# Attention slots and loads from unit 12 on placed later, and a planner that counts outstanding DMAs

## The chip, the cores and the metric

One core of a Trainium2 chip runs the kernel. The metric is the device time of one execution in microseconds (us). Several executions are timed; their median stands for the kernel. One further execution is recorded by the hardware profiler, and all views of the profile are of that one.

## The reference

Windowed attention with sink keys, and on its output a two-layer feed-forward net with a gate:

```python
scores = (q @ k.T) / 8           # batch 4, heads 8, sequence 768, head size 64
keep   = (key < 4) | (0 <= query - key < 128)
a      = softmax(where(keep, scores, -1e9))
x      = (a @ v)                 # heads side by side: 3072 tokens x 512
h      = x @ w_in                # 512 -> 2048
g      = h * sigmoid(beta * h)   # beta per column of h
out    = g @ w_out               # 2048 -> 512
```

All inputs and the output are float32; the kernel computes its products in bf16.

## The kernel before, in words

The 3072 tokens are cut into 8 **blocks** of 384 tokens (`NT`, `TT`). A block needs the attention of 4 **units**: unit n is one pair of heads for one half (384 queries) of one sequence. Units 4T to 4T+3 belong to block T, so there are 32 units, 0 to 31 (`NU`).

One unit goes through these steps:

- `load(n)` (line 392) reads q, k and v from DRAM into float32 staging tiles. All these loads are issued by SP, but for two at the start. Units 0 to 11 load one half in one way; units 12 to 15 load one half with 256-byte runs (six DMAs of 96 KB); from unit 16 on (`WHOLE`) a load fetches both halves of a pair of heads at once (six DMAs of 192 KB), so that only every second group of four units loads.
- `cast(n)` (line 438): GpSimd (POOL) casts q and k to a bf16 tile `qk16` (3 buffers) and v into `v_aug`. From unit 12 on (`XBAR`) a DMA transpose, issued by SP (line 453), turns `qk16` into `qkT`. Units before 12 are transposed by TensorE.
- scores by TensorE into `s_ps` (line 554; the sink keys at line 490), exponentials by ACT, masks by DVE, attention times v by TensorE (lines 593 and 604), division by DVE into `o_norm` (line 614). The sink keys are copied out of `qkT` by ACT (line 481).
- `transpose_out(n)` (line 619): from unit 12 on another DMA transpose of SP (line 623) puts `o_norm` into `xT`, the input of the feed-forward net.

A block's feed-forward part has 16 tiles of hidden columns. For each, TensorE makes 4 matmuls over `xT` (line 651, one for each of the block's four units), ACT a tanh (line 659) and DVE the gate (line 672). Then 48 projections (line 679; 16 for each of 3 groups of 128 tokens) go into a PSUM bank, ACT (once DVE) copies it to `out_sb` (line 687), and SP stores it (line 694).

**What sets the order.** The program is first written down in steps s = -6, -5, ...: each step has one hidden tile of a block, three projections of the block before, and whichever attention steps fall there. `FIRST[n]` is the step at which unit n starts; its scores come 3 steps later, its attention 5. `casts` gives the step of each cast, and calls of `load` are tied to certain casts. Every instruction becomes a node with a duration (`busy`, `lag`) and the nodes it depends on. `Prog.order` then plans: at each turn it takes, over all five engines, the node that could start first by these durations, among the next 160 nodes of an engine (40 for SP). So an instruction can be drawn ahead of others in the written order when the planner thinks that it will be ready. For DMAs the planner keeps one clock `dma_free`: a transfer occupies it for `lag` (size by a rate) and is landed 2000 ns after. `emit` writes each engine's instructions in the planned order, with semaphore waits. On the chip every engine, and SP's queue with all loads, transposes and stores in it, goes through its list strictly in that order.

Of the kernel before, what the change touches and what calls it, by code (L numbers as in the profile page):

```python
# [9 lines left out]
B, H, S, D = 4, 8, 768, 64  # L10
# [7 lines left out]
TT = 384  # L18
# [22 lines left out]
S_END = S_PIPE + (NT - 2) * NM  # L41

FIRST = {4: -6, 5: -4, 6: -2, 7: 1, 8: 22, 9: 26, 10: 30, 11: 34}
FIRST.update({n: 42 + 4 * (n - 12) for n in range(12, NU)})

XBAR, WHOLE = 12, 16

# [23 lines left out]
class Prog:  # L71
# [10 lines left out]

    ENGINES = ("pe", "act", "dve", "gp", "sp")
    AHEAD = {"pe": 160, "act": 160, "dve": 160, "gp": 160, "sp": 40}
    FIRST_DMA = 2000.0

    def __init__(self):
        self.nodes = []
# [64 lines left out]
    def order(self):  # L153

        for n in self.nodes:
            n.open = len(n.preds)
            for p in n.preds.values():
                p.succs.append(n)
        free = dict.fromkeys(self.ENGINES, 0.0)
        left = {e: [n for n in self.nodes if n.eng == e] for e in self.ENGINES}  # L160
        head = dict.fromkeys(self.ENGINES, 0)
        can = {e: [n for n in left[e] if n.open == 0] for e in self.ENGINES}
        placed = []
        dma_free = self.FIRST_DMA

        def best(e):
            q = left[e]
            while head[e] < len(q) and q[head[e]].place is not None:
                head[e] += 1
            if head[e] == len(q):  # L170
                return None
            last = q[min(head[e] + self.AHEAD[e], len(q) - 1)].id
            c = [n for n in can[e] if n.id <= last]
            if not c:
                return None
            n = min(c, key=lambda n: (max(n.ready, free[e]) + n.give, n.id))
            return max(n.ready, free[e]), n

        while len(placed) < len(self.nodes):
            found = [(*b, e) for e in self.ENGINES if (b := best(e)) is not None]  # L180
            start, n, e = min(found, key=lambda f: (f[0], f[1].id))
            free[e] = start + n.busy
            if n.dma is None:
                n.done = start + n.busy + n.lag
            else:

                dma_free = max(dma_free, start + n.busy) + n.lag
                n.done = dma_free + 2000.0
            n.place = start
            can[e].remove(n)  # L190
            placed.append(n)
            for s in n.succs:
                s.open -= 1
                early = s.id in n.soft or s.eng == e and not n.dma
                s.ready = max(s.ready, start + n.busy if early else n.done)
                if s.open == 0:
                    can[s.eng].append(s)
        return placed
# [64 lines left out]
def bass_streamingllm_window__then__act_swish_beta_kernel(  # L263
# [75 lines left out]
    def dve(t):  # L339
        return {"busy": t, "lag": 140.0}  # L340

    def transfer(size, rate):
        return {"busy": 500.0, "lag": size / rate}


    def select(out_ap, in_ap, patt, cmp, fill, base, cm, r, w):
# [45 lines left out]
    def load(n, v_queue="sp"):  # L392
        b, hp, half, pb = place(n)
        t0 = half * TT
        if n < XBAR:
            for name, src in (("q", q), ("k", k)):
                s = src[b, 2 * hp:2 * hp + 2, t0:t0 + TT, :].rearrange("h (p c) d -> p h (c d)", c=3)
                d = stage[name][pb][:, :, 3 * half:3 * half + 3, :].rearrange("p h c d -> p h (c d)")
                op("sp", lambda e, d=d, s=s: e.dma_start(d, s),  # L399
                   w=[(name + "_stage", pb, half, 0), (name + "_stage", pb, half, 1)],  # L400
                   dma=f"{name}{pb}_{half}", line=n < WHOLE, **transfer(2 * TT * D * 4, 329))
        halves = (0, 1) if n >= WHOLE else (half,)
        first, size = (0, 6) if n >= WHOLE else (3 * half, 3)
        for name, src in (("q", q), ("k", k), ("v", v)):
            if name != "v" and n < XBAR:
                continue
            for hh in range(2):
                s = src[b, 2 * hp + hh, 128 * first:128 * (first + size), :].rearrange(
                    "(c p) d -> p c d", p=128)
                op(v_queue, lambda e, hh=hh, s=s, name=name: e.dma_start(  # L410
                    stage[name][pb][:, hh, first:first + size, :], s),
                   w=[(name + "_stage", pb, x, hh) for x in halves],
                   dma=f"{name}{pb}_{half}{hh}", line=n < WHOLE and v_queue == "sp",
                   **transfer(size * 128 * D * 4, 220))

    w_in_src = moe_w_in.rearrange("(c p) f -> p c f", p=128)
    w_out_src = moe_w_out.rearrange("(m p) n -> p m n", p=128)
# [10 lines left out]
    def load_w(i):  # L428
        view, src, _ = w_piece(i)
        op("sp", lambda e: e.dma_start(view, src), w=[("wst", i % NW)], dma=f"w{i % NW}",  # L430
           line=True, **transfer(1 << 19, 389))

    def cast_w(i):
        view, _, dst = w_piece(i)
# [3 lines left out]
    def cast(n):  # L438
        _, _, half, pb = place(n)
        z = n % NQK  # L440

        def view(name):
            return stage[name][pb][:, :, 3 * half:3 * half + 3, :].rearrange("p h c d -> p c h d")

        for x, name in enumerate("qk"):
            op("gp", lambda e, x=x, name=name: e.tensor_copy(qk16[z][:, x, :, :, :], view(name)),  # L446
               r=[(name + "_stage", pb, half, hh) for hh in range(2)], w=[(name + "16", z)],
               busy=451.0, lag=100.0)
        op("gp", lambda e: e.tensor_copy(v_aug[pb][:, 3 * half:3 * half + 3, :, 0:D], view("v")),  # L449
           r=[("v_stage", pb, half, hh) for hh in range(2)], w=[("v_aug", pb, half)], busy=451.0,  # L450
           lag=100.0)
        if n >= XBAR:
            op("sp", lambda e: e.dma_start_transpose(
                qkT[pb][:, half, :, :].rearrange("p w (c x) -> p (w c) x", c=3),
                qk16[z][:, :, :, :, :].rearrange("p w c h d -> p (w c h d)")),
               r=[("q16", z), ("k16", z)], w=[("qkT", pb, half)], dma=f"t{pb}{half}",
               **transfer(2 * TT * 256, 150))


    def transpose_in(n, bank=tr_ps, name_of="tr", eng="dve"):  # L460
# [158 lines left out]
    def transpose_out(n, bank=tr_ps, name="tr", eng="dve"):  # L619
        _, hp, _, _ = place(n)  # L620
        z, T = n % NON, n // 4
        if n >= XBAR:
            op("sp", lambda e: e.dma_start_transpose(
                xT[:, hp, T * TT:(T + 1) * TT].rearrange("p (c x) -> p c x", c=3),
                o_norm[z][:, :, :, :].rearrange("p m h d -> p (m h d)")),
               r=[("o_norm", z)], w=[("xT", T, hp)], dma=f"x{z}", **transfer(TT * 256, 150))
            return
        bank16 = bank[:, :].bitcast(BF16)
        with P.together("pe"):
            for m in range(3):  # L630
                op("pe", lambda e, m=m: nc.tensor.transpose(
                    bank16[:, m * 128:(m + 1) * 128],
                    o_norm[z][:, m, :, :].rearrange("p h d -> p (h d)"), ident[:, :]),
                   r=[("o_norm", z), "ident"], w=[name], **pe(128))
        op(eng, lambda e: (e.copy if eng == "act" else e.tensor_copy)(
            xT[:, hp, T * TT:(T + 1) * TT], bank16[:, 0:TT]),
           x=[name], w=[("xT", T, hp)], **(act(TT) if eng == "act" else dve(275.0)))
# [40 lines left out]
    def project(T, t, m, bank, name, eng="act"):  # L678
        op("pe", lambda e: e.matmul(bank, g[T % 2][:, m, t * 128:(t + 1) * 128],  # L679
                                    w_out16[:, m, :], start=(m == 0), stop=(m == NM - 1)),  # L680
           r=[("g", T % 2, m), ("w_out", m // 2)], w=[name], **pe(NOUT))
        if m == NM - 1:
            z = n_out[0] % 4
            n_out[0] += 1

            if eng == "act":
                op("act", lambda e: e.activation(out_sb[z][:, :], bank, AF.Copy, bias=0.0,  # L687
                                                 scale=0.5),
                   x=[name], w=[("out_sb", z)], **act(NOUT))
            else:  # L690
                op("dve", lambda e: e.tensor_scalar(out_sb[z][:, :], bank, 0.5, None, ALU.mult),
                   x=[name], w=[("out_sb", z)], **dve(600.0))
            row = T * TT + t * 128
            op("sp", lambda e: e.dma_start(out[row:row + 128, :], out_sb[z][:, :]),
               r=[("out_sb", z)], dma=f"o{z}", **transfer(128 * NOUT * 4, 389))


    constants()
# [69 lines left out]
    for s in range(-6, S_END + NM):  # L768
# [27 lines left out]
        if s in casts:  # L796
            n = casts[s]
            cast(n)
            if n >= XBAR and n % 8 >= 4 and n + 4 < NU:
                load(n + 4)  # L800
        if s == FIRST[5] + 2:
            for x in range(4, 8):
                cast_w(x)
# [11 lines left out]
            load_w(15)  # L815
            load(12)
            load(13)
            load(14)
            load(15)
        if s == 34:  # L820

            first = {0: (mask_a[:, :], MASK_A), 1: (mask_b[:, 128:512], MASK_B)}
# [72 lines left out]
```

## Time and profile before

| | us |
|---|---|
| three timed runs | 233.91, 234.16, 235.10; median 234.16 |
| profiled execution, first to last instruction (span) | 234.5 |
| TensorE (PE) busy | 219.4 |
| ACT busy | 144.3 |
| DVE busy | 135.2 |
| POOL busy | 74.3 |
| bytes moved by DMA | 39.76 MB, 170 GB/s on average |

The profile gives the span of its execution; it has no other time of it, and the timed runs lie on both sides of that span. A page and its views are read as follows. A line such as `L679 PE MATMUL acc<-w_out,g` is a group of instructions of line 679 of the kernel on TensorE, which write `acc` and read `w_out` and `g`. `PE a <- DMA b: 2.3, 1, 2.3` in the list of waits says that TensorE's instruction a waited for the transfer b, 2.3 us in total, once, 2.3 us at the longest. In a timeline a line gives the start, the duration, the engine and the instruction; SPq is SP's DMA queue, whose durations are those of issuing, not of transferring. In a table of windows each line gives a stretch, its length, the busy time of PE, weight loads, DVE, ACT and POOL with the number of instructions, then TensorE's granted clock, the DMA engines' share and the GB/s that they moved.

### The profile page before, as it was taken

The page shows a single profiled execution, that of the slowest core. Times are in us where ns is not written, and L with a number is a line of the kernel's source. Part 1 is how long each engine was busy: PE and PEld are TensorE (multiplying, and loading weights), DVE is VectorE, ACT ScalarE, POOL GpSimd, SP SyncE. Part 2 cuts the span into 40 slices and gives each one's busy share as a digit, 9 for nine tenths or more (in the row PEclk, how much of TensorE's full clock was granted, in tenths as well). Part 3 has the DMA queues.
Part 4 walks back from the last instruction along what each step waited for, and adds up shares of the span by engine and source line. Part 5 has one row for each costly group of instructions (what it writes and reads, how often), then busy time and mean ns, then how long its engine had stood idle before and what let it go on. Part 6 is the DMA issues. An engine that isn't in the chain of part 4 may idle for free.

```text
span 234.5 us, 4406 instructions
## 1 busy us (share of the span) xinstructions
PE 219.4 (94%) x1690; PEld 119.7 (51%) x1714; DVE 135.2 (58%) x261; ACT 144.3 (62%) x249; POOL 74.3 (32%) x134
## 2 busy tenths in 40 slices
PE   4996989999969999999999999999999999999994
PEld 2653545555434555544555555555555555555541
DVE  5374999699632645632667547766656665343300
ACT  2385887697506674755875669767775874555421
POOL 7677777598313223214115343410000000000000
PEclk9999999999997999999999999999999999999999
DMA  6999999999699999998999886842220112111012
GB/s 158 269 373 264 318 328 227 321 388 197 147 212 226 177 218 255 203 231 201 215 232 214 182 169 164 160 84 64 62 64 17 45 20 62 45 48 45 19 71 89
DMA packets 96084, 39.76 MB, mean 170 GB/s; under 512 B 82736, under 2 KB 88896, under 8 KB 96064
## 3 DMA queue, kind: packets, MB, share of 16 engines
q1 hardware_dynamic: 93888, 39.07, 71.0%
q10 hardware_dynamic: 1632, 0.40, 0.8%
q8 instruction: 13, 0.21, 0.4%
q0 software_dynamic: 544, 0.02, 0.2%
q14 instruction: 7, 0.06, 0.1%
HBM read 27.30 MB, written 6.29 MB: 143 GB/s over the span
## 4 chain that ended last, share of the span: by engine, by line
PE 68%; SPq 20%; DMA 8%; issue 2%; POOL 1%; ACT 0%; POOLq 0%; ACTq 0%
PE acc L679 32%; PE h_ps L651 27%; SPq L410 13%; DMA v_stage<-in_v_dram 6%; SPq L399 4%; PE s_ps L554 4%; PE s_ps L604 3%; SPq L430 3%; DMA qkT<-qk 1%; PE s_ps L490 1%; PE s_ps L593 1%; PE h_ps L679 1%; POOL v_aug L449 0%; ACT out_sb L687 0%; POOL qk L446 0%
## 5 line engine op out<-in xcount | busy, mean ns | idle before, releaser
L679 PE MATMUL acc<-w_out,g 128*128 128x512 bf16 x345 | 94.0, 382 | 1.3 <-issue 0.5
L659 ACT ACTIVATE th<-h_ps,beta_half 128x384 f32<-128x384 f32 x104 | 58.9, 581 | 37.7 <-PE h_ps L651 35.8
L651 PE MATMUL h_ps<-xT,w_in 128*128 128x384 bf16 x416 | 79.4, 326 | 0.3 <-issue 0.2
L672 DVE SCALAR_TENSOR_TENSOR g<-th,h_ps 128x384 bf16<-128x384 f32 x104 | 56.0, 552 | 33.6 <-ACT th L659 32.0
L651 PEld LDWEIGHTS h_ps<-xT,w_in 128*128 128x128 bf16 x416 | 39.5, 98 | 30.3 <-DVE g L672 1.5
L679 PEld LDWEIGHTS acc<-w_out,g 128*128 128x128 bf16 x368 | 34.7, 98 | 34.0 <-issue 3.8
L570 DVE TENSOR_TENSOR E<-E,mask_all 128x1536 bf16<-128x1536 bf16 x20 | 19.4, 972 | 29.0 <-ACT E L561 29.0
L561 ACT ACTIVATE E<-s_ps 128x1536 bf16<-128x1536 f32 x20 | 28.9, 1447 | 5.9 <-PE s_ps L554 5.7
L446 POOL CAST qk<-q_stage 128x384 bf16<-128x384 f32 x32 | 18.3, 571 | 33.9 <-DMA qkT<-qk 33.3
L449 POOL CAST v_aug<-v_stage 128x384 bf16<-128x384 f32 x32 | 16.6, 529 | 35.0 <-PE s_ps L604 24.7
L687 ACT ACTIVATE out_sb<-acc 128x512 f32<-128x512 f32 x23 | 13.6, 597 | 14.6 <-PE acc L679 14.2
L651 PE MATMUL acc<-xT,w_in 128*128 128x384 bf16 x96 | 19.1, 327 | 2.6 <-DVE g L672 2.0
L604 PEld LDWEIGHTS s_ps<-v_aug,E 128*128 128x128 bf16 x384 | 17.1, 97 | 5.3 <-ACT E L524 0.7
L604 PE MATMUL s_ps<-v_aug,E 128*128 128x65 bf16 x384 | 19.4, 193 | 0.5 <-ACT E L524 0.4
L614 DVE TENSOR_TENSOR o_norm<-s_ps,rden 128x384 bf16<-128x384 f32 x32 | 17.8, 558 | 2.2 <-DVE rden L612 0.5
L446 POOL CAST qk<-k_stage 128x384 bf16<-128x384 f32 x32 | 18.3, 572 | 2.4 <-DMA k_stage<-in_k_dram 1.7
L659 ACT ACTIVATE th<-acc,beta_half 128x384 f32<-128x384 f32 x24 | 13.7, 580 | 5.9 <-PE acc L651 5.3
L672 DVE SCALAR_TENSOR_TENSOR g<-th,acc 128x384 bf16<-128x384 f32 x24 | 12.9, 547 | 3.8 <-ACT th L659 3.7
L524 ACT ACTIVATE E<-s_ps 128x768 bf16<-128x768 f32 x16 | 12.9, 809 | 2.2 <-PE s_ps L517 2.1
L475 DVE COPY qkT<-s_ps 128x768 bf16<-128x768 bf16 x10 | 9.5, 954 | 5.7 <-PE s_ps L468 5.7
L651 PEld LDWEIGHTS acc<-xT,w_in 128*128 128x128 bf16 x96 | 8.1, 98 | 8.5 <-DVE g L672 3.4
L481 ACT COPY k_sink<-qkT 64x4 bf16<-64x4 bf16 x32 | 6.1, 190 | 10.0 <-DVE qkT L475 9.0
(64 smaller groups left out, 155.0 us busy)
## 6 DMA issues: line engine op xcount, KB each, us to landing
out_dram<-out_sb SPq DMA_DIRECT2D x24, 256.0 KB, 2.3
q_stage<-in_q_dram SPq DMA_DIRECT2D x28, 192.0 KB, 4.2
k_stage<-in_k_dram SPq DMA_DIRECT2D x28, 192.0 KB, 4.2
wst<-in_moe_w_in_dram SPq DMA_DIRECT2D x8, 512.0 KB, 6.3
wst<-in_moe_w_out_dram SPq DMA_DIRECT2D x8, 512.0 KB, 9.1
v_stage<-in_v_dram SPq DMA_DIRECT2D x16, 192.0 KB, 4.2
v_stage<-in_v_dram SPq DMA_DIRECT2D x28, 96.0 KB, 5.3
q_stage<-in_q_dram SPq DMA_DIRECT2D x8, 96.0 KB, 3.3
```

What stands on the lines that cost most here:

```text
L410: op(v_queue, lambda e, hh=hh, s=s, name=name: e.dma_start(stage[name][pb][:, hh, first:first + size, :], s), w=[(name + "_stage", pb, x, ...
L446: op("gp", lambda e, x=x, name=name: e.tensor_copy(qk16[z][:, x, :, :, :], view(name)), r=[(name + "_stage", pb, half, hh) for hh in range ...
L449: op("gp", lambda e: e.tensor_copy(v_aug[pb][:, 3 * half:3 * half + 3, :, 0:D], view("v")), r=[("v_stage", pb, half, hh) for hh in range(2 ...
L561: op("act", lambda e: e.activation(E[z][:, :, :, :].rearrange("p c h x -> p c (h x)"), s_ps[:, :, :].rearrange("p (h b) x -> p h (b x)", h ...
L570: op("dve", lambda e: e.tensor_tensor(both, both, mask_all[:, half, :].unsqueeze(1).to_broadcast([128, 2, 768]), ALU.mult), r=[("E", z, 0) ...
L604: last=(x == len(kbs) - 1): e.matmul(av_ps[:, at + hh * D1:at + hh * D1 + D1], E[z][:, c, h2, col:col + 128], v_aug[pb][:, kb, hh, :], sta ...
L614: op("dve", lambda e: e.tensor_tensor(o_norm[o][:, :, :, :].rearrange("p m h d -> p (m h) d"), src[:, :, 0:D], rden[z][:, :].unsqueeze(2). ...
L651: op("pe", lambda e: e.matmul(bank, w_in16[:, c, m * 128:(m + 1) * 128], xT[:, c, T * TT:(T + 1) * TT], start=(c == 0), stop=(c == 3)), r= ...
L659: op("act", lambda e: e.activation(th[i % 3][:, :], bank, AF.Tanh, bias=0.0, scale=beta_half[:, m:m + 1]), x=[name], r=["beta"], w=[("th", ...
L672: op("dve", lambda e: e.scalar_tensor_tensor(g[T % 2][:, m, :], th[i % 3][:, :], 1.0, bank, ALU.add, ALU.mult), r=[("th", i % 3)], x=[name ...
L679: op("pe", lambda e: e.matmul(bank, g[T % 2][:, m, t * 128:(t + 1) * 128], w_out16[:, m, :], start=(m == 0), stop=(m == NM - 1)), r=[("g", ...
L687: op("act", lambda e: e.activation(out_sb[z][:, :], bank, AF.Copy, bias=0.0, scale=0.5), x=[name], w=[("out_sb", z)], **act(NOUT))
```

## The change

`FIRST` moves units 12 to 31 three steps later. The loads of units 14 and 15 and of all later pairs move from one place, or from the cast of the unit four before, to the cast of the unit two before (for the pairs that load in advance, a step of half a group later). The planner's DMA model is altered: the first DMA starts at 1300 instead of 2000, no more than 7 DMAs may be outstanding (a DMA starts only when the seventh before it has landed), issuing takes 525 ns for a load, 1400 for a transpose of q and k and 1250 for a transpose out, and the rates are others. No instruction's shape or number is touched.

```diff
-FIRST.update({n: 42 + 4 * (n - 12) for n in range(12, NU)})
+FIRST.update({n: 45 + 4 * (n - 12) for n in range(12, NU)})
...
-    FIRST_DMA = 2000.0
+    FIRST_DMA = 1300.0
+    DEPTH = 7
...
         dma_free = self.FIRST_DMA
+        landing = []
...
             n = min(c, key=lambda n: (max(n.ready, free[e]) + n.give, n.id))
-            return max(n.ready, free[e]), n
+            start = max(n.ready, free[e])
+            if n.dma is not None and len(landing) >= self.DEPTH:
+                start = max(start, landing[-self.DEPTH])
+            return start, n
...
                 n.done = dma_free + 2000.0
+                landing.append(n.done)
...
-    def transfer(size, rate):
-        return {"busy": 500.0, "lag": size / rate}
+    def transfer(size, rate, issue=525.0):
+        return {"busy": issue, "lag": size / rate}
...
    load, units 0 to 11, q and k:   rate 329 -> 300
    load, the others:               rate 220 -> 250
    load_w:                         rate 389 -> 380
    transpose of q and k:           rate 150 -> 240, issue 1400
    transpose out:                  rate 150 -> 280, issue 1250
    store of the output:            rate 389 -> 350
...
             cast(n)
-            if n >= XBAR and n % 8 >= 4 and n + 4 < NU:
-                load(n + 4)
+            if n in (12, 13):
+                load(n + 2)
+            if n >= XBAR + 2 and n % 8 in (6, 7, 0, 1) and n + 2 < NU:
+                load(n + 2)
...
             load(12)
             load(13)
-            load(14)
-            load(15)
```

More of the change, by code (lines that the diff above doesn't have):

```diff
@@ L400, in load @@
                    w=[(name + "_stage", pb, half, 0), (name + "_stage", pb, half, 1)],
-                   dma=f"{name}{pb}_{half}", line=n < WHOLE, **transfer(2 * TT * D * 4, 329))
+                   dma=f"{name}{pb}_{half}", line=n < WHOLE, **transfer(2 * TT * D * 4, 300))
         halves = (0, 1) if n >= WHOLE else (half,)
@@ L413, in load @@
                    dma=f"{name}{pb}_{half}{hh}", line=n < WHOLE and v_queue == "sp",
-                   **transfer(size * 128 * D * 4, 220))
+                   **transfer(size * 128 * D * 4, 250))
     w_in_src = moe_w_in.rearrange("(c p) f -> p c f", p=128)
@@ L430, in load_w @@
         op("sp", lambda e: e.dma_start(view, src), w=[("wst", i % NW)], dma=f"w{i % NW}",
-           line=True, **transfer(1 << 19, 389))
+           line=True, **transfer(1 << 19, 380))
     def cast_w(i):
@@ L456, in cast @@
                r=[("q16", z), ("k16", z)], w=[("qkT", pb, half)], dma=f"t{pb}{half}",
-               **transfer(2 * TT * 256, 150))
+               **transfer(2 * TT * 256, 240, 1400.0))
     def transpose_in(n, bank=tr_ps, name_of="tr", eng="dve"):
@@ L625, in transpose_out @@
                 o_norm[z][:, :, :, :].rearrange("p m h d -> p (m h d)")),
-               r=[("o_norm", z)], w=[("xT", T, hp)], dma=f"x{z}", **transfer(TT * 256, 150))
+               r=[("o_norm", z)], w=[("xT", T, hp)], dma=f"x{z}", **transfer(TT * 256, 280, 1250.0))
             return
@@ L694, in project @@
             op("sp", lambda e: e.dma_start(out[row:row + 128, :], out_sb[z][:, :]),
-               r=[("out_sb", z)], dma=f"o{z}", **transfer(128 * NOUT * 4, 389))
+               r=[("out_sb", z)], dma=f"o{z}", **transfer(128 * NOUT * 4, 350))
     constants()
```

## The prediction

> **What bounds the kernel now.** I read the view of cores first (one core, clock 0.992), then the page: TensorE is busy for 219.4 of 234.5 us, so what can be won is idle or slowed TensorE time. TensorE's waits name the largest piece, and its timeline places it.
>
> ```profile
> span 234.5 us, 4406 instructions
> PE 219.4 (94%) x1690; PEld 119.7 (51%) x1714; DVE 135.2 (58%) x261; ACT 144.3 (62%) x249; POOL 74.3 (32%) x134
> ```
>
> ```profile
> PE s_ps L490 <- DMA qkT<-qk: 2.3, 1, 2.3
> PE h_ps L509 <- DVE far_b L382: 2.0, 1, 2.0
> ```
>
> ```profile
> 67.53 0.33 PE L631 MATMUL s_ps<-ident,o_norm 128*128 128x128 bf16 x3
> 70.13 0.34 PE L490 MATMUL s_ps<-qkT,k_sink 128*128 128x384 bf16 x1 [2.27 <-DMA qkT<-qk]
> ```
>
> TensorE runs dry at 67.86 us and waits 2.27 us for the transposed q and k of unit 12. The 2.03 us wait is in the start-up, where nothing is edited. Windows of 1 us show what follows (the number behind POOL's count is the granted clock):
>
> ```profile
> 69.00:70.00 1.00, 0.00 (x0) 0.00 (x0) 0.00 (x0) 0.00 (x0) 0.00 (x0) 1.00 0.97 209
> 70.00:71.00 1.00, 0.87 (x3) 0.36 (x4) 0.00 (x0) 0.49 (x1) 0.77 (x2) 0.72 1.27 245
> 71.00:72.00 1.00, 1.00 (x5) 0.16 (x3) 0.00 (x0) 0.00 (x0) 0.19 (x1) 0.50 1.27 216
> 72.00:73.00 1.00, 1.00 (x10) 0.51 (x10) 0.00 (x0) 0.15 (x1) 0.00 (x0) 0.50 1.35 220
> 73.00:74.00 1.00, 1.00 (x4) 0.36 (x3) 0.00 (x0) 1.00 (x1) 0.00 (x0) 0.57 1.29 230
> ```
>
> The clock falls to half for 3.4 us; what is lost is 0.28 + 0.50 + 0.50 + 0.43 = 1.71 us. After that TensorE is busy in every window to the end. Why the transpose was late stands in SP's queue: it is issued at 66.60 us, behind 26 loads, without having waited itself.
>
> ```profile
> 45.02 2.98 SPq L410 DMA_DIRECT2D q_stage<-in_q_dram  x2
> ...
> 65.48 1.07 SPq L410 DMA_DIRECT2D q_stage<-in_q_dram  x2
> 66.60 1.32 SPq L453 DMA_TRANSPOSE qkT<-qk  x1
> 67.97 1.17 SPq L410 DMA_DIRECT2D k_stage<-in_k_dram  x2
> ...
> 91.76 2.08 SPq L453 DMA_TRANSPOSE qkT<-qk  x1
> 93.89 1.26 SPq L623 DMA_TRANSPOSE xT<-o_norm  x1
> ```
>
> The last view is the chain that ended last; TensorE's own spacing is read from it, 3.45/16 = 0.216 us for a projection matmul and 0.65/4 = 0.1625 us for a hidden one (the page's 382 and 326 ns are latencies that overlap).
>
> ```profile
> 219.65 0.65 PE h_ps L651 x4
> 220.30 3.45 PE acc L679 x16
> ```
>
> **The change part by part.** No instruction is added or removed; the edits alter the planner's numbers and the program order, and so each engine's written-out order. I compared the orders of the two kernels; positions below are counted in them.
>
> *The wait that goes.* In the new order the transpose of unit 12 (T12; likewise for other units) stands behind the loads of units 12 and 13 only. These end at 57.80 us in SP's timeline, and POOL's cast of unit 12 ends at 57.38, so T12 is issued at about 57.9 and lands 3.5 us later (as at 66.60), at 61.4. TensorE asks for it after five more projection matmuls than before: 67.86 + 5 x 0.216 = 68.9. The wait and its clock drop go: 2.27 + 1.71 = 3.98 us. With nothing else the span is 234.5 - 4.0 = 230.5.
>
> *What is late next.* Block 3's hidden matmuls (its first reads all of xT for units 12 to 15) started at 111.2 us, behind 42 projections of block 2 that fill TensorE from 100.1 on. Now they stand earlier while the attention slots stand three steps later, and the last of their four inputs, the output transpose of unit 15 (xT15), stands further back in SP's queue. When TensorE asks: from 67.86 to the fourth of these matmuls the new order has 75 projections (16.2), 67 hidden matmuls (10.9), scores of 5 units at 0.44 (2.2), 4 sink scores at 0.17 (0.7), and attention of 5 units (4 x 0.53 + 0.36 = 2.5): 32.5 us. The same sum over the old order from T12's wait to the end gives 157.4 against 161.2 - 1.7 = 159.5 measured, 1.3% of small waits; so 32.9, and TensorE asks at 100.75.
>
> When xT15 lands: behind T12 come 6 loads, T13, 6 loads, T14. With 0.53 us for a half-pair load and 1.3 for a transpose (rows between 54.65 and 66.60) that is 57.9 + 12 x 0.53 + 3 x 1.3 = 68.2. Between there and xT15 stand 24 whole-pair loads, T15 to T18 and T20, xT12 to xT14, and 5 output stores. Before, 24 such loads, 5 such transposes and 3 stores took SP from 65.48 to 93.89, 28.4 us, without waiting for an engine. Adding 3 x 1.24 and 2 x 0.57 gives 33.3: xT15 issued at 101.5. Its landing took 3.1 to 4.1 us between 94 and 98: 104.6 to 105.6. That is one end. The other comes from the bytes: 24 x 0.197 + 5 x 0.197 + 4 x 0.098 + 5 x 0.262 = 7.4 MB, and some 0.45 MB still under way at 68.2; the window from 72 to 96 moved 226 GB/s at a DMA share of 1.29. The old stretch moved 6.5 MB in 28.4 us, 229 GB/s; 7.85 MB at that take 34.3 us: landing at 102.5. The rows are near each other; I take 103.5, a wait of 2.75 us (1.75 to 4.85).
>
> On the way T13 and T14 wait for POOL's casts with the next loads queued behind them: cast 13 ended at 59.6, SP gets there at 62.4; cast 14 ended at 63.6 and slips by one transpose, SP gets there at 66.9. No loss.
>
> *Sum.* What TensorE has left then: 272 x 0.216 + 317 x 0.1625 + 15 units' scores (6.6) + 8 sink scores (1.4) + 15 units' attention (6.8) = 125.1, with 1.3% 126.7; and 3.1 us from its last matmul to the end (231.4 to 234.5). Span 103.5 + 126.7 + 3.1 = 233.3, so 1.2 us less than 234.5.
>
> *Block 4* is asked for 24.8 us after block 3 (191 instructions by the same spacing). xT19 is 19 loads, 4 qk transposes, 4 output transposes and 3 stores behind xT15: 5.7 MB, 24.9 us at 229 GB/s. So the second wait is near nothing, up to 2 us if SP keeps 0.73 us per load. In blocks 5 to 7 the last attention ends 5.3 to 5.7 us before the hidden matmul that needs it; normalising (about 1.3) and a transpose (2.6 median landing) take 3.9. Nothing, with at most 0.5 us a block.
>
> *Waits moved onto ACT.* ACT copies unit 16's sink keys when T16 has landed, ahead of the next tanh, which frees a PSUM bank for TensorE. ACT gets there at about 85.9; T16 is issued near 81.5 and lands 5.7 later (as T14 did): 87.2. Up to 1.3 us, and for T17 up to 2. TensorE has no cover for it, but it is not additional: it arrives so much later at a block 3 that waits for xT15 anyway. Without that wait it would cost its own 0 to 2 us.
>
> *Edits at nothing.* FIRST_DMA, rates, issue times and DEPTH act only through the order. Casts move on POOL, which is 32% busy. TensorE's order before 45 us is reshuffled too; the waits it could change there are 0.57, 0.76, 0.42, 0.49, 0.49, 0.32 and 0.40, so I bound it at 1 us either way, hidden behind block 3's wait if that stands.
>
> [...] The row is the half clock right after 2.27 us of idleness. [...] The second row is 226 GB/s at loads that write 256-byte runs. [...]
>
> **The rivals.** *A, full gain: 230.5 to 231.4.* Transfers keep up. For it: between 30 and 35 us the DMAs moved 336 GB/s, and the new order spreads loads between transposes. Against: those 336 were mostly longer rows, and from 65 to 90, where loads and transposes ran as they will here, it was 210.
>
> *B, slower: the new wait halves the clock as the old one did.* It needs one wait at block 3 (or 4) of about the length that did it before, 2.27. Price up to 1.71, less what falls into the wait itself. From a wait of 2.3 us on nothing is won (2.3 + 1.7 = 4.0); from 3.5 on it is slower by over 0.5%. With the late end, 4.85 + 1.7, span 234.5 - 4.0 + 6.55 = 237.0; at 4.1 + 1.7, 236.3. [...]
>
> *C, the change doesn't do what it says: T12 still late,* for a cast that slips; 234.5. Against: 7 us of slack.
>
> **How the numbers follow.** Forecast (wait comes back, clock stays) 0.48; A 0.24; B 0.25; C 0.03. The runs' median, 234.16, is 0.34 below the profiled span; the page gives no other time of that execution. So 233.3 - 0.3 = 233.0 us for the run; block 4's possible share moves me to 233.2. Range 230.0 (A, 230.5 less 0.34 and a little) to 236.0 (B with a wait of 4.1), leaving out the longer waits of B. Half a percent, about what a measurement here can tell from no change, is 1.17 us. Faster: A and 0.18 of the forecast, 0.42. Same: 0.24 of the forecast, 0.12 of B, and C, 0.39. Slower: 0.13 of B, and 0.06 of the forecast for a second wait at blocks 4 to 7, 0.19. The forecast's own range, without those, is 103.5 replaced by 102.5 and 105.6: 232.0 to 235.1.
>
> **What would show it.** Right: no TensorE wait on qkT near 68 us; T12 issued near 58; a wait of h_ps on the DMA of xT near 101, of 1.7 to 4.9 us; SP issuing without pause from 58 to 101. Wrong: xT15 landed before 100.7 (A); half clock behind 101 (B); waits in blocks 5 to 7, or small waits in the first 45 us grown by over 1 us.

## The result, and the profile after

The changed kernel takes 243.13 us (median of four executions, 241.53 to 244.38) beside 234.03 us (233.84 to 235.1) for the kernel before: a ratio of 1.0383, 95% interval 1.0324 to 1.0441. It is slower by 9 us. The profiled execution is the one of 244.09 us; its span is 242.4 us. Ratios leave out executions over 1.5% above the fastest of the same kernel; one of these, the run cover's at a granted clock of 0.66, is also the reason why that kernel's profile comes from a second run.

The page's first lines:

```profile
span 242.4 us, 4427 instructions
PE 224.0 (92%) x1714; PEld 119.7 (49%) x1714; DVE 136.7 (56%) x261; ACT 144.9 (60%) x249; POOL 71.0 (29%) x134
```

TensorE is busy for 4.6 us more than before, with the same instructions. Half clock explains some 3.4 us of it: it lasts 10.24 us in all (below), 3.41 before. The rest can't be read off, since the profile of before holds 1690 of the 1714 matmuls. The list of TensorE's waits from 60 us on (what waits, for whom, total us, times, longest):

```profile
PE h_ps L657 <- DMA xT<-o_norm: 5.2, 2, 2.9
PE s_ps L560 <- DVE o_norm L620: 0.3, 1, 0.3
```

The wait on unit 12's transpose (T12) is gone. In its place stand two waits of hidden matmuls on output transposes. TensorE's timeline shows that they are those of blocks 3 and 4:

```profile
101.80 0.84 PE L657 MATMUL h_ps<-xT,w_in 128*128 128x384 bf16 x3
105.00 0.99 PE L657 MATMUL h_ps<-xT,w_in 128*128 128x384 bf16 x5 [2.36 <-DMA xT<-o_norm]
...
131.07 0.65 PE L657 MATMUL h_ps<-xT,w_in 128*128 128x384 bf16 x3
134.61 1.78 PE L657 MATMUL h_ps<-xT,w_in 128*128 128x384 bf16 x5 [2.89 <-DMA xT<-o_norm]
```

Each time three matmuls go ahead on the inputs that have landed, and the fourth waits for the block's last unit (xT15, xT19). Windows of 1 us show the clock behind the waits (the number behind POOL's count):

```profile
106.00:107.00 1.00, 1.00 (x8) 0.39 (x9) 0.90 (x2) 0.98 (x2) 0.00 (x0) 0.74 0.75 139
107.00:108.00 1.00, 1.00 (x4) 0.46 (x3) 0.21 (x2) 0.94 (x1) 0.72 (x2) 0.50 1.01 191
...
134.00:135.00 1.00, 0.39 (x2) 0.23 (x3) 0.00 (x0) 0.00 (x0) 0.00 (x0) 0.50 1.21 257
...
139.00:140.00 1.00, 1.00 (x5) 0.45 (x4) 0.82 (x1) 0.58 (x1) 0.01 (x1) 0.50 1.32 260
140.00:141.00 1.00, 1.00 (x6) 0.47 (x4) 0.55 (x1) 0.30 (x2) 0.00 (x0) 0.69 1.14 324
```

Half clock lasts 3.41 us behind the first wait and 6.83 us behind the second. SP's queue tells why the transposes were late (start, time to issue, instruction):

```profile
57.07 1.32 SPq L459 DMA_TRANSPOSE qkT<-qk  x1
...
102.55 1.25 SPq L629 DMA_TRANSPOSE xT<-o_norm  x1
...
119.69 1.22 SPq L629 DMA_TRANSPOSE xT<-o_norm  x1
120.95 0.58 SPq L416 DMA_DIRECT2D k_stage<-in_k_dram  x1
121.58 1.13 SPq L416 DMA_DIRECT2D v_stage<-in_v_dram  x2
122.75 1.59 SPq L416 DMA_DIRECT2D q_stage<-in_q_dram  x2
124.38 1.74 SPq L416 DMA_DIRECT2D k_stage<-in_k_dram  x2
126.17 1.73 SPq L416 DMA_DIRECT2D v_stage<-in_v_dram  x2
127.94 0.84 SPq L416 DMA_DIRECT2D q_stage<-in_q_dram  x1
128.82 1.51 SPq L629 DMA_TRANSPOSE xT<-o_norm  x1
```

T12 goes at 57.07 us, 0.8 us before the forecast. xT15 goes at 102.55; xT19 (the last line) has ten whole-pair loads between it and xT18. Compared with the kernel before neither is late; there SP issued xT15 and xT19 later still:

```profile
105.73 1.21 SPq L623 DMA_TRANSPOSE xT<-o_norm  x1
...
132.28 1.26 SPq L623 DMA_TRANSPOSE xT<-o_norm  x1
```

What moved further is TensorE's question. Before, the hidden matmuls of blocks 3 and 4 began at 111.22 and 137.60 us:

```profile
111.22 1.46 PE L651 MATMUL h_ps<-xT,w_in 128*128 128x384 bf16 x8
...
137.60 1.46 PE L651 MATMUL h_ps<-xT,w_in 128*128 128x384 bf16 x8
```

Now they begin at 101.80 and 131.07, so 9.4 and 6.5 us earlier, while the two transposes are issued only 3.2 and 3.5 us earlier. They are late for the place that the planner gave to their readers. The chain that ended last goes through xT19:

```profile
127.23 1.35 ACT E L567
128.82 5.74 DMA xT<-o_norm
134.61 1.78 PE h_ps L657 x5
```

This view leaves out its shortest pieces, and it infers what released a transfer from the event that came last. Here it names ACT, but ACT is not what held xT19: DVE had written `o_norm` for unit 19 by 124.99 us, and SP came to the transpose when it had issued the loads ahead of it, at 128.78.

### The profile page after: what moved, and what is told of

It reads as the page before. It is cut to its first block, busy times and chain, and to the rows that moved or that the text cites. A ratio compares the mean times of both kernels' runs of the same rounds, so it can differ in the third digit from the quotient of the medians.

```text
span 242.4 us, 4427 instructions
## 1 busy us (share of the span) xinstructions
PE 224.0 (92%) x1714; PEld 119.7 (49%) x1714; DVE 136.7 (56%) x261; ACT 144.9 (60%) x249; POOL 71.0 (29%) x134
## 4 chain that ended last, share of the span: by engine, by line
PE 72%; DVE 11%; DMA 7%; ACT 4%; SPq 3%; issue 1%; POOL 0%; ACTq 0%; POOLq 0%
PE acc L685 29%; PE h_ps L657 26%; PE s_ps L610 4%; DMA xT<-o_norm 3%; DVE g L678 3%; DVE E L541 3%; PE s_ps L560 3%; PE acc L657 3%; DVE qkT L481 2%; SPq L416 2%; DMA k_stage<-in_k_dram 2%; DMA v_stage<-in_v_dram 2%; ACT E L530 2%; PE h_ps L685 1%; PE s_ps L474 1%
## 5 line engine op out<-in xcount | busy, mean ns | idle before, releaser
L685 PE MATMUL acc<-w_out,g 128*128 128x512 bf16 x368 | 99.5, 382 | 0.0
L657 PE MATMUL h_ps<-xT,w_in 128*128 128x384 bf16 x416 | 84.4, 336 | 5.3 <-DMA xT<-o_norm 5.2
L665 ACT ACTIVATE th<-h_ps,beta_half 128x384 f32<-128x384 f32 x104 | 60.1, 581 | 44.1 <-PE h_ps L657 41.7
L657 PEld LDWEIGHTS h_ps<-xT,w_in 128*128 128x128 bf16 x416 | 40.8, 100 | 40.1 <-DMA xT<-o_norm 6.3
L685 PEld LDWEIGHTS acc<-w_out,g 128*128 128x128 bf16 x368 | 33.9, 98 | 32.7 <-issue 4.3
L452 POOL CAST qk<-q_stage 128x384 bf16<-128x384 f32 x32 | 16.5, 517 | 39.9 <-DMA q_stage<-in_q_dram 18.7
L455 POOL CAST v_aug<-v_stage 128x384 bf16<-128x384 f32 x32 | 16.1, 519 | 22.2 <-PE s_ps L610 11.8
L452 POOL CAST qk<-k_stage 128x384 bf16<-128x384 f32 x32 | 17.2, 539 | 17.4 <-DMA k_stage<-in_k_dram 16.7
```

What stands on the lines that cost most here:

```text
L657: op("pe", lambda e: e.matmul(bank, w_in16[:, c, m * 128:(m + 1) * 128], xT[:, c, T * TT:(T + 1) * TT], start=(c == 0), stop=(c == 3)), r= ...
L665: op("act", lambda e: e.activation(th[i % 3][:, :], bank, AF.Tanh, bias=0.0, scale=beta_half[:, m:m + 1]), x=[name], r=["beta"], w=[("th", ...
```

## The experiments

The letters here are those of the experiments, not the prediction's. Theory **W**: the new order puts output transposes behind loads on a transfer queue that the planner believes faster than it is; blocks 3 and 4 wait for them, and each wait brings a stretch at half clock. Rivals: **D**, the transfers are behind as a whole, wherever the matmuls stand; **E**, the reshuffled first 45 us cost the time (TensorE idles 6.38 us between 5 and 60 us, 4.54 before); the later **slots and loads** cost it; **C**, the clock alone costs it. Ratios are against the kernel before, run beside each on the same chip; its medians there were 234.54, 235.35 and 234.24 us.

**late_xt: the planner told that output transposes land 4 us later.**

```diff
-                n.done = dma_free + 2000.0
+                n.done = dma_free + 2000.0 + n.late
...
-  dma=f"x{z}", **transfer(TT * 256, 280, 1250.0))
+  dma=f"x{z}", late=4000.0, **transfer(TT * 256, 280, 1250.0))
```

> The changed kernel, but the planner is told that an output transpose lands 4 us later than it reckons. So block 3's hidden matmuls stand 8 us of TensorE work later, block 4's 4 and block 5's 7; T12 stays early. Theory W (TensorE waits at blocks 3 and 4 for output transposes that the planner believed landed, and each wait halves the clock): both waits and the half clock go, span about 232.5, time 232 to 234. Rival D (the transfers as a whole have become too slow; the wait only shows first at blocks 3 and 4): the waits come back one block later, time 239 or more. Rival E (the new order of the first 55 us is what costs): that order is kept here, time 241 or more.

Measured 233.54 us, ratio 0.9962 (0.9931 to 0.9994); span 231.3. The list of TensorE's waits from 60 us on is one line, with no transpose in it:

```profile
PE h_ps L659 <- DVE g L680: 0.3, 1, 0.3
```

xT19 goes at 118.63 us with thirteen whole-pair loads fewer ahead of it, block 4's matmuls stand 3.8 us of TensorE work later, and the DMAs moved 206 GB/s from 83 to 109 us and 199 from 109 to 135, no faster than in the changed kernel (206 from 83 to 105, 202 from 105 to 134.6). So the transfers are not behind as a whole: D falls. TensorE's order is the changed kernel's up to block 3, so the new order of the first 45 us was kept: E falls as the main cause.

**planner_only: the kernel before with the new DMA model alone.**

```diff
+    DEPTH = 7
...
-  **transfer(size * 128 * D * 4, 220)
+  **transfer(size * 128 * D * 4, 250)
```

> The kernel before with the new DMA model alone: slots from step 42 and loads as before. Block 3's hidden matmuls stand as early as in the changed kernel, but T12 stands behind 24 loads and not 12. Theory W: xT15 has 24 loads and 6 transposes behind T12, is issued near 99.4 and lands near 102.5, when TensorE asks (102.4): wait of 0 to 1 us at block 3, about 1 at block 4, time 234 to 238. If the slots' shift of three steps is what costs, 234 or less. If the planner alone does the harm, 241 to 244.

Measured 243.87 us, ratio 1.0363 (1.0315 to 1.0411). My figure for W missed: I had taken the slots to be part of the cause. The model alone does all the harm, at other places: T12 is as late as before (65.39 us), four waits on qkT of 0.35 to 1.45 us follow, and one at block 4, for an xT19 that goes at 130.71:

```profile
134.41 1.58 PE L657 MATMUL h_ps<-xT,w_in 128*128 128x384 bf16 x5 [4.83 <-DMA xT<-o_norm]
```

Block 4 thus goes on at the same time as in the changed kernel (134.61), and from there to the end it takes 108.0 us (107.8). In the two orders nearly the same stands ahead of xT19 on SP: 42 whole-pair loads and 11 transposes of q and k here, 43 and 12 there. That accounts for the two times being so near; that like amounts on SP make like landings was not tested by itself.

**slots_loads_only: the kernel before with the later slots and loads, the old DMA model kept.**

```diff
-FIRST.update({n: 42 + 4 * (n - 12) for n in range(12, NU)})
+FIRST.update({n: 45 + 4 * (n - 12) for n in range(12, NU)})
...
-            if n >= XBAR and n % 8 >= 4 and n + 4 < NU:
-                load(n + 4)
+            if n in (12, 13):
+                load(n + 2)
...
```

> The kernel before with the slots three steps later and the loads moved, but the old DMA model. Block 3's hidden matmuls stand where they stood before, T12 behind 26 loads as before, and TensorE asks for it 1.1 us of work later. Theory W: the wait on T12 shrinks from 2.3 to about 1.2, no waits at blocks 3 and 4: time 232 to 234. If the shift of slots is what costs: 238 or more.

Measured 235.54 us, ratio 1.0042 (1.0002 to 1.0081), 1.5 us above W's figure: of waits on transfers, 0.97 us for an xT at 110.05 and 0.21 for a qkT are left. The slots and loads cost 0.4%, not 4%. It has 47 whole-pair loads ahead of xT19, more than the changed kernel's 43, and no wait at block 4, whose matmuls stand 9 us of TensorE work later.

**half_bytes: the changed kernel, whole-pair loads fetching only their first half** (the second half of each such pair's q, k and v is not loaded).

```diff
+                part = 3 if n >= WHOLE else size
...
-                    stage[name][pb][:, hh, first:first + size, :], s),
+                    stage[name][pb][:, hh, first:first + part, :], s),
```

> The changed kernel in the same order, but the loads of whole pairs (from unit 16 on) fetch only the first half of each sequence; the other half of the staging tiles keeps what was there, so that part of the computation uses old data. Theory W with the transfer rate as the limit of SP's queue: 2.4 MB less before xT15, which is issued near 96 and lands near 99, before TensorE asks at 102.6: no wait at block 3 or 4, span 232 to 235. Rival I (SP's issuing itself is the limit, whatever the size): xT15 is still issued at about 102 and the waits stay, span 240 to 243.

One execution, 233.52 us, span 231.8, with no wait of TensorE after 60 us. The instructions and their order on SP are unchanged, yet xT15 goes at 98.61 and xT19 at 122.38 us (102.55 and 128.82 in the changed kernel). xT19 also lands 2.5 us after its issue there, and 5.7 in the changed kernel. SP was held back by what it had already sent, not by its own issuing. The loads' runs of 256 bytes were halved with their bytes; the run does not tell these two apart, and it is a single execution.

**late_b4: late_xt's delay for block 4's transposes alone.**

```diff
-  dma=f"x{z}", late=4000.0, **transfer(TT * 256, 280, 1250.0))
+  dma=f"x{z}", late=4000.0 if T == 4 else 0.0, **transfer(TT * 256, 280, 1250.0))
```

> The changed kernel, in which the planner takes block 4's output transposes alone (xT16 to xT19) to land 4 us later than its model says. Block 3's hidden matmuls stay where the change put them, block 4's move back by 3.7 us of TensorE work. Theory W (each wait on an output transpose costs its own length and half of the stretch at half clock that follows it): block 3's wait of 2 to 3 us with 3.4 us at half clock stays, block 4's 2.9 us and the 3.4 us lost in 6.8 us at half clock go: 243.1 - 2.9 - 3.4 = 236.8, taken as 235.5 to 238. Rival D (the queue is simply behind, and a wait removed at block 4 comes back at a later transpose): 240 to 243. Rival L (block 4 carries all of the loss, block 3's wait is absorbed later): 233 to 235.

Measured 238.07 us, ratio 1.0144 (1.0079 to 1.0209), 0.07 us above W's range. Block 3's wait stays (2.32 us at 105.08, then 3.4 us at half clock); block 4's is gone, for xT19 goes at 125.05 with six loads ahead of it in place of ten. Of the 4.2% between the changed kernel and late_xt, block 4 carries 2.4 points and block 3, once block 4 is mended, 1.8 (each to within some 0.9).

**early_old: late_xt with the old order of the first 45 us** (limit and new rates only from unit 12's loads on, and only for transposes the new rates).

```diff
-            if n.dma is not None and len(landing) >= self.DEPTH:
+            if n.dma is not None and n.id >= self.deep and len(landing) >= self.DEPTH:
...
+            P.deep = len(P.nodes)
             load(12)
```

> The planner of before for everything up to unit 12's loads, so that the first 45 us keep the old order; from there the slots at 45, the moved loads, the limit of seven and the new times of the transposes, the old rates of the other transfers, and xT taken to land 4 us later. Theory W: no wait on an xT or qkT transpose after 60 us, full clock, 232.5 to 234, the same as the run late_xt within 0.7 us. Theory E (the new order of the first 45 us costs the 1.8 us by which TensorE's early waits grew): 231 to 232, 1.5 us or more below late_xt's 233.5.

Measured 233.54 us, ratio 0.9943 (0.9907 to 0.9979), span 231.5: the same as late_xt. The early order is worth nothing that shows. This is the fastest version of the study, but its interval and late_xt's overlap.

**after_old_start: the changed kernel with the old order of the first 45 us.** As in early_old the planner of before orders everything up to unit 12's loads; from there all of the changed kernel's numbers hold, its load rate of 250 too, and there are no 4 us.

> The changed kernel with the old order of the first 45 us: block 3's hidden matmuls stand after 83.3 us of TensorE work and block 4's after 108.4, as in the changed kernel (83.7 and 108.4). Theory W: the end is set by when xT15 and xT19 land, so time saved early is given back as longer waits there: 241.5 to 243.5. Theory E (the early order's 1.8 us adds to the waits): 240 to 241.4. If it falls below 239, the early order takes part in the waits at blocks 3 and 4, which neither theory says.

Measured 243.5 us, ratio 1.0343 (1.0259 to 1.0427). In the profile (span 239.1) TensorE waits for ScalarE and VectorE ahead of block 3 (1.50 and 0.76 us at 95 to 97 us, with half clock behind them) and comes to block 3 when xT15 has landed; ScalarE had itself waited 2.85 us for a qkT at 95.00; at block 4 it waits as before:

```profile
133.58 0.99 PE L659 MATMUL h_ps<-xT,w_in 128*128 128x384 bf16 x5 [2.52 <-DMA xT<-o_norm]
```

The ratio can't be told from the changed kernel's (1.0383, 1.0324 to 1.0441), though early waits are shorter. With early_old beside late_xt, E falls: the 1.8 us that it named do not show in either pair.

**old_rates: the changed kernel with the planner's old rates; the limit and the new issue times stay.**

```diff
-                   **transfer(size * 128 * D * 4, 250))
+                   **transfer(size * 128 * D * 4, 220))
...
-               **transfer(2 * TT * 256, 240, 1400.0))
+               **transfer(2 * TT * 256, 150, 1400.0))
...
-  **transfer(TT * 256, 280, 1250.0))
+  **transfer(TT * 256, 150, 1250.0))
```

> The changed kernel with the planner's old transfer rates (220 for loads in place of 250, 150 for transposes in place of 240 and 280, 329 and 389 for the rest), but its limit of seven and its longer issue times kept. Block 3's hidden matmuls then stand after 88.2 us of TensorE work (83.7 in the changed kernel, 91.9 in late_xt) and xT15 is issued one place earlier; block 4's stay at 108.2. Theory W with the rates as the part that misled the planner: no wait at block 3 or under 1 us, at block 4 one of 0 to 3 us with 3.4 us at half clock: 234 to 239. Rival (the limit of seven or the longer issue times misled it, the rates didn't): 241 to 244.

Measured 234.73 us, ratio 1.0005 (0.9967 to 1.0042), with no wait on a transfer after 60 us. The rates are what misled the planner. Which of them was not told apart: those of loads, of both transposes, of weights and of stores went back together.

**no_limit: the changed kernel with DEPTH at a thousand.**

```diff
-    DEPTH = 7
+    DEPTH = 1000
```

> The changed kernel with the limit of seven lifted to a thousand, so that the planner issues loads ahead again; its new rates and issue times kept. Unit 12's transpose then stands behind more loads, as in the kernel before, block 3's hidden matmuls after 85.9 us of TensorE work and block 4's after 106.6. Theory W (the rates misled the planner, whatever the limit): the wait on unit 12's transpose of some 2 us comes back and waits at block 3 or 4 stay: 238 to 244. Rival (the limit is what does the harm): 233 to 236.

Measured 247.12 us, ratio 1.0573 (1.0472 to 1.0675): further up than W's figure, and the opposite of the rival. With the new rates the limit helps by some 4 us. Without it T12 is late again (66.35 us, a wait of 1.23), and beside 1.43 us at block 3 and 3.41 at block 4 TensorE waits 3.37 us at 91.37 for ScalarE, which I hadn't foreseen: ScalarE had waited 4.21 us for a qkT at 89.68, so this too is the queue's.

**cover and cover_again: the changed kernel with matmuls that do nothing of use in the places of the two waits.**

```diff
+    COVER = {3 * NM: 14, 4 * NM: 24}
...
+            for _ in range(COVER.get(i, 0)):
+                cover(i)
             for c in range(3 if i < 2 else 0, 4):
```

> The changed kernel, in the same order, with extra matmuls (128x384, 0.164 us each) put ahead of the first hidden group of block 3 (14, 2.3 us) and of block 4 (24, 3.9 us), into the same bank, which the real group then starts afresh; the planner counts them as no time. TensorE works where it waited. Theory C (half clock comes from TensorE's idleness): full clock after block 3, 1.7 us won there; block 4 is asked for at 130.0, with the cover at 133.9, and xT19 lands at 134.6 as before, so a wait of 0 to 1 us stays and the 6.8 us at half clock, 3.4 us lost, go: 238.5 to 240.5. Rival (the half clock has another source, the traffic of transfers for one): it comes at 105 and 134 as before, 242 to 245.

> The kernel of the run cover once more, for a profile at full clock: its timed executions took 240.1, 241.0 and 241.0 us of span at clocks of 1.0, 0.998 and 0.993. Theory C with a cover of the right size: no wait above 1 us before blocks 3 and 4, clock 0.998 or more, and the span is then 239 to 241 because xT19's landing at 134 to 135 us sets block 4's start whatever the clock does before it. Rival O (the cover is too long: the transposes land before it ends, and its 6.2 us are paid as work): xT15 or xT19 lands 1 us or more before the cover's end, and the last wait is none. Rival S (something later than block 4 takes the time back): a stretch after 145 us with 1 us or more of idle TensorE that the changed kernel's profile doesn't have.

cover took 242.69 us, ratio 1.0347 (1.0261 to 1.0433): theory C had 238.5 to 240.5, and misses. The second run, with 243.81 us and a span of 241.9 (239 to 241 expected), gives the profile. The clock is full (1.00 in the mean, against 0.979 and 0.986 in the changed kernel's two profiles), so in this kernel idle TensorE is what halves it; but the time stays. TensorE's timeline around block 4:

```profile
129.72 4.06 PE L674 MATMUL h_ps<-xT,w_in 128*128 128x384 bf16 x24
133.62 0.65 PE L657 MATMUL h_ps<-xT,w_in 128*128 128x384 bf16 x3
135.20 0.99 PE L657 MATMUL h_ps<-xT,w_in 128*128 128x384 bf16 x5 [0.93 <-DMA xT<-o_norm]
...
146.06 0.32 PE L496 MATMUL s_ps<-qkT,k_sink 128*128 128x384 bf16 x1 [1.17 <-ACT E L567]
```

TensorE was at block 4 1.35 us earlier (129.72 against 131.07) and still could not start before 135.2: xT19's landing sets that. And behind the changed kernel's half clock this one meets the next wait: from 141 to 160 us TensorE is idle for 1.75 us, in the changed kernel for none. The view names ScalarE, but ScalarE had waited 1.89 us for a qkT itself (at 144.04), so it is a transfer again, and rival S's stretch after 145 us came in part. From block 4's fourth matmul to the end it takes 106.7 us, in the changed kernel 107.8: there 6.0 us of that stretch run at half clock, 3.0 us lost, and they are worth 1.1. By after_old_start, with full clock in that stretch and 105.5 us, they are worth 2.3; its order is a little different.

**after_again: the changed kernel, profiled once more.**

> The changed kernel once more, for a second profile: its four executions took spans of 239.8 to 242.6 us at clocks of 0.979 to 0.993. Theory W: waits on xT15 and xT19 of 2 to 3.5 us each again, block 4's the longer; the half clock that follows them 3.4 or 6.8 us in all, so that the span lies between 239.5 and 242.6. If one of the waits is under 1 us and the span is still above 239.5, the waits don't carry the loss and theory W is in doubt.

242.43 us, span 240.7, clock 0.986. The waits are the same, 2.35 and 2.92 us, at 104.78 and 134.11; half clock lasts 3.4 us each time. W's waits hold. From block 4's fourth matmul to the end it takes 106.6 us, as long as cover_again at full clock.

## Why the prediction was wrong

The prediction was 233.2 us, the measurement 243.13. In its own terms, for the profiled executions (span 233.3 forecast, 242.4 measured):

| step | forecast | measured | adds to the span |
|---|---|---|---|
| T12 issued; no wait on qkT near 68 | 57.9 | 57.07, none | 0 |
| TensorE asks for xT15 | 100.75 | 102.64 | hidden by the wait |
| xT15 lands, block 3 goes on | 103.5 (102.5 to 105.6) | 105.0 | 1.5 |
| from there to block 4's question | 24.8 | 26.7 | 1.9 |
| wait at block 4 | near nothing, up to 2 | 2.89 | 2.9 |
| from there to the end | 105.0 | 107.8 | 2.8 |
| sum | | | 9.1 |

**Right**: the wait that goes, and the one that takes its place, in place and about in size (2.75 forecast, 2.36). Of its cause one half: block 3's matmuls do stand earlier. But xT15 does not stand "further back in SP's queue": 24 whole-pair loads are ahead of it, 30 before. The issue by SP (101.5 forecast, 102.55) was the better of the two ends for xT15's landing, the bytes at 229 GB/s the worse. That 229 counts what was issued in the stretch of before; what the view of windows has as moved there, from 65.48 to 93.89 us, is 220. TensorE asked 1.9 us late, about the 1.8 us that its early waits grew by.

**The step that failed** is block 4's: "5.7 MB, 24.9 us at 229 GB/s. So the second wait is near nothing". From xT15's landing to xT19's it took 29.6 us, 4.7 more. In them the DMAs moved 202 GB/s and 5.98 MB: 0.3 MB more and a rate 12% lower than the 229 taken from the one stretch of before. The mean hides two parts. xT19 was issued 26.3 us after xT15, 1.4 more than 24.9. And it took 5.74 us to land, where xT15 took 2.41: 3.3 us for which the sum had no term. Right ahead of xT15 stand two transposes of q and k, ahead of xT19 ten whole-pair loads, and with the same ten at half the bytes (half_bytes) it landed in 2.5. TensorE then asked at 131.7 and got its input at 134.6. By that landing alone block 4 starts 6.3 us later than forecast (134.6 against 100.75 + 2.75 + 24.8 = 128.3). What TensorE did before it hardly matters: in after_again, cover_again and after_old_start block 4 went on at 134.1, 135.2 and 133.6, with full clock or half and with a wait at block 3 or none. So the first three terms of the table are one: the queue's. late_b4 shows it from the other side, and half_bytes that it shrinks with the size of the loads.

**The clock**: rival B's mechanism came, at both blocks, 3.41 and 6.83 us at half clock. B's price was too low in length (it had one wait) and too high in worth: behind block 3 the loss is hidden by the wait at block 4, and behind block 4 full clock wins 1.1 to 2.3 us of 3.0. The forecast added nothing for the clock behind its wait of 2.75 us. No run shows that a wait of such a length costs only itself: those of 2.32 us (late_b4), 2.36 and 2.89 us (the changed kernel) and 2.35 and 2.92 us (after_again) were followed by half clock, and one of 2.52 us (after_old_start) was not.

**The small terms**: "bound it at 1 us either way" for the first 45 us was short, 1.8 us, but after_old_start and early_old show it worth nothing. Blocks 5 to 7 were costed at nothing and had no wait on a transfer. ACT did wait for qkT (3.58 us at 103.10, 1.50 at 95.42), but TensorE did not wait for ACT; in after_old_start, cover_again and no_limit it did.

**Span and time**: I set the profiled span of before beside the runs' median as if they were of one kind. In every execution of this study that lists both, the time is 1.5 to 2.1 us above the span. So a span of 233.3 would have been some 235.1, and before's profiled execution (span 234.5, clock 0.992) was one of the longer. Of 50 executions of before that ran beside these kernels, 43 had a clock above 0.993 and a median span of 232.7; the other seven had 234.9. By that clock a stretch at half clock was in few of them, and removing the wait wins less than the 3.98 us of the profile: late_xt and early_old, which have no wait left, win 0.4 and 0.6%. Rival A's span of 230.5 to 231.4 is nearly what they reached (231.3 and 231.5), and it was the planner's order that kept the change from it.

What stays open: which of the rates misled the planner most, and whether it is the loads' bytes or their number of short runs that hold SP back.

## What to carry to other kernels

Where a planner orders the queues, a rate that is too high pulls the consumer forward to a time at which nothing has landed; that did the harm here, for fewer loads stood ahead of xT19 than before (43 against 46). It also lets loads go ahead that a truer plan puts behind: 13 of them in late_xt, where the wait went. When a change moves a wait to the next consumer, do the sum for the one after it with the same care, take the queue's rate from several stretches of the trace, the lowest among them, and add how long a transfer takes to land behind the loads that stand right ahead of it. In this kernel the wait at block 4 had a nearly fixed end (133.6 to 135.2 us in the changed kernel, after_again, cover_again and after_old_start): keeping the clock up before it won nothing that shows (cover's ratio 1.0347 beside 1.0383) as long as SP's order stayed.

## What the runs showed of the hardware

In the profiles of this study, cover's first apart, the granted clock fell from 1.00 to 0.50, for 3.41 us (before, the changed kernel's block 3) or for 6.83 us (its block 4), and the gap's length doesn't decide alone. A wait of 2.52 us (after_old_start) left the clock at full, and single waits of 0.97 (slots_loads_only), 1.39 (late_b4), 1.45 (planner_only) and 1.59 us (old_rates) did too, while 1.50 us, with 0.76 us more within the next 1.0 us (after_old_start), brought 3.4 us at half clock. What goes with it here is the place of the gap. In the changed kernel the clock changes at 106.48, 109.89, 133.79 and 140.61 us: all on one grid of 3.413 us (from drop to drop 27.31 us, 8 times that). Cut on this grid, each window's TensorE busy time (second number) goes with the clock of the next. The changed kernel:

```profile
103.07:106.48 3.41, 1.48 (x12) 0.73 (x13) 0.49 (x1) 2.02 (x5) 1.92 (x4) 1.00 0.76 177
106.48:109.89 3.41, 3.41 (x11) 1.52 (x10) 2.24 (x4) 2.04 (x3) 0.96 (x2) 0.50 0.65 138
...
133.79:137.20 3.41, 2.59 (x14) 1.10 (x15) 0.72 (x2) 1.18 (x3) 0.51 (x1) 0.50 1.25 273
137.20:140.61 3.41, 3.41 (x11) 1.47 (x11) 2.10 (x3) 2.01 (x2) 0.51 (x1) 0.50 1.28 253
```

after_old_start, whose gap of 2.52 us a window's edge cuts into 1.90 and 0.62:

```profile
129.55:132.96 3.41, 1.51 (x17) 0.70 (x14) 0.75 (x2) 0.60 (x1) 0.96 (x2) 1.00 1.05 145
132.96:136.37 3.41, 2.79 (x20) 1.21 (x21) 1.11 (x2) 2.20 (x5) 0.51 (x1) 1.00 1.05 246
```

In the profiles of this study (cover's first apart), between 10 and 225 us, every full-clock window with 1.93 us of idleness or more (1.93 is the changed kernel's from 103.07 us) is followed by half clock (ten windows in seven profiles), and every one with 1.90 or less (1.90 is after_old_start's from 129.55 us) by full clock. A window at half clock with 0.82 us of idleness (the changed kernel's from 133.79 us) was followed by another at half, those with 0.75 or less (late_b4's from 106.2 us, with 0.34, is one) by full clock. The ends of matmuls are modelled, so the two bounds are near figures.

Loads and transposes together moved 192 to 206 GB/s in stretches of 22 to 30 us between 57 and 135 us, in late_xt as in the changed kernel; in half_bytes, with no wait left, it was 163 from 83 to 109 us and 161 from 105 to 134.
